# Soft-capped attention into an attention mixture: pairs of heads taken two by two, with one exponential for each two

## The chip, the core and the metric

The kernel runs on one NeuronCore of a Trainium2 chip. A core has five engines that run side by side, each through its own instructions in order: TensorE (PE in the profile, its weight loads PEld), VectorE (DVE), ScalarE (ACT), GpSimd (POOL) and SyncE (SP, which here issues most of the DMAs). They meet through semaphores. Matmul results go to PSUM, which has eight banks of 512 fp32 values on each of 128 partitions; everything else lies in SBUF. The metric is the device time of one execution in microseconds (us).

## The reference

There are two stages. The first is ordinary attention over 8 batches and 12 heads with 448 tokens and head size 64, whose scores are capped by a tanh. The second takes its result as x (448 tokens, 768 wide for each batch), runs four causal attention experts of head size 64 over it, and mixes the two experts that a gate picks for each token.

```python
scores = scale * np.matmul(q, k.transpose(0, 1, 3, 2))
scores = cap * np.tanh(scores / cap)                    # cap = 30
attn = np.exp(scores - np.max(scores, axis=-1, keepdims=True))
x = (attn / attn.sum(-1, keepdims=True)) @ v            # heads side by side
...
logits = x @ w_gate                                     # top 2 of 4 experts, softmax of the two
for e in range(E):
    q = x @ wq[e]; k = x @ wk[e]; v = x @ wv[e]
    a = softmax(causal(scale * (q @ k.transpose(0, 2, 1))))
    ye = a @ v @ wo[e]
    out += mask_e * w_e * ye
```

## The kernel before

The work of the first stage is cut into **pairs** of heads: 8 batches of 6 pairs make 48 pairs, numbered through. Pairs 42 to 47, the last batch, are computed for their first 320 tokens as pairs 42 to 47, and for the remaining 128 tokens of all six as two more units, 48 and 49, of three pairs each. The scores of a pair are seven blocks of 448 columns: keys 0 to 383 in three chunks of 128 for each of the two heads, which makes six blocks, and a **tail** with the last 64 keys of both heads.

For each pair, PE writes these blocks into PSUM (`heads`, L854, for the chunks, where the two heads run side by side on half the rows each; `tails`, L864). ACT applies the tanh from PSUM into an SBUF buffer `yp` (`tanh`, L907): three blocks from the **score tile** X, then two from Y, then two from Y again. The names of the three are X, Y1 and Y2. Then one exponential runs in place over all seven blocks, 3136 columns (`expo`, L919). PE multiplies the result by v (`pv`, L934 for the tail and L942 for the chunks), in four windows of 128 tokens and two PSUM banks; v carries a column of ones, so that the sum of the exponentials comes out beside the product. DVE divides (L965, L968). The pair's result is transposed, by PE or, from pair 36 on, by DMA, and stands as x for the second stage.

PSUM's eight banks are divided by hand: tile X has three, tile Y has two, and three banks, A0 to A2 (`AUX`), serve all other matmul results, one group of matmuls for each bank until DVE has read it. The second stage may use the banks of X where these are idle.

The second stage of batch b runs while ACT works on the pairs of the next batch. PE computes values and gate logits (L1088), keys and queries (L1096); POOL picks the experts and builds a mask (`g_`, `mB`), which a DMA transposes (`mT`) and DVE multiplies onto the queries (`qm`, L1170). `b_score` then writes scores for two experts into X, and ACT takes their exponential, 1024 columns, from there (L1301). This comes twice for a batch, at fixed pairs (`exps`): 5 and 6 pairs after the batch's end, or 4 and 6 for the last two of the seven batches handled so. Behind it come the product with the values (L1351), the weighting (L1366), the sum over experts on POOL (L1376), a transpose, and the output projection with `wo` (L1413), which `ob` carries to the output. The eighth batch's second stage, the end of the kernel, has code of its own, `last`.

What sets the order is a **planner** inside the kernel. `Graph.op` records each operation with its engine, a cost and its reads and writes; ACT's operations of the first stage form a fixed chain; `Graph.dues` gives every other operation a due time from that chain, and `Graph.solve` lists the operations of all engines by due time, cost and free banks, with corrections by hand or by search in the table `RANKS`. The result is one fixed order for each engine; on the chip, only semaphores decide when an instruction starts. `Group(banks)` stands for a result that needs one of these banks; `takes` and `frees` say which score banks an operation occupies or gives back.

The main loop goes over the pairs and calls, for pair p, in this order: X of p; Y1 of p; then the exponential of p - 1, what the second stage has due, PV and transpose of p - 1; then Y2 of p. So ACT runs tanh X, tanh Y1, exponential of the pair before, tanh Y2, and round again. `yp` has four buffers of seven blocks.

Of the kernel before, what the change touches and what calls it, by code (L numbers as in the profile page):

```python
# [26 lines left out]
        136: 93, 174: 305, 290: -418,  # L27
    }),
    (27.5, {
        507: 475,  # L30
    }),
    (67.5, {
        678: -572, 692: 231, 735: -81, 738: -31, 741: 513, 841: 473, 1112: 748, 1167: -284,
    }),
    (87.5, {
        716: 497, 727: -643, 760: -112, 767: -1037, 862: 1282, 888: 375, 919: 264,
    }),
    (127.5, {
        1092: 467, 1196: 214, 1239: -453, 1249: 345, 1267: 323, 1277: 281, 1398: -60, 1401: 289,
        1405: 243, 1449: -132, 1535: 337, 1537: 820,  # L40
    }),
    (147.5, {
        1338: 97, 1345: 117, 1355: 477, 1387: -702, 1413: 186, 1525: 119, 1548: -196,
    }),
    (167.5, {
        1600: 205, 1607: 294,
    }),
# [7 lines left out]
    }),  # L55
    (254.5, {
        2520: -331, 2577: -265, 2635: -902, 2645: 2133, 2659: 128, 2667: 486, 2678: 522, 2702:
        -188, 2703: -340, 2706: -238, 2713: -937, 2729: -581, 2766: 2204, 2788: 297,
# [3 lines left out]
TURN = 2.2  # L62
SAIL = 1.1
SHIP = 1.25
BEGIN = {"POOL": 0.8, "DVE": 0.9, "SP": 0.8, "ACT": 0.8, "PE": 1.25}
NWARM = 6
KEEP = 8
# [4 lines left out]
PDUE = 2.793  # L72
PSTEP = 11.594
# [3 lines left out]
KD = 34  # L77
NFILL = 35
# [10 lines left out]
class Group:  # L89


    def __init__(self, banks, hold=0.0):
        self.banks = banks
        self.hold = hold
        self.bank = None
        self.last = None


class Graph:
# [66 lines left out]
    def dues(self, when):  # L166


        for o in reversed(self.ops):
            d = INF  # L170
            if o.own is not None:
                d = o.own if not isinstance(o.own, tuple) else when[o.own[0].idx] + o.own[1]
            d = min(d, when.get(o.idx, INF))
            for s, late in o.succ:
                d = min(d, s.due - self.gap(o, s, late) - (0.1 if s.eng != o.eng else 0.0))
            o.due = d
        for o in self.ops:
            if o.opens:
                o.grp.due = o.due
            if o.grp is not None and not o.opens and o.grp.hold:  # L180
                o.due = min(o.due, o.grp.due + o.grp.hold)

    def solve(self, when, banks, lent):
# [21 lines left out]
        def pick(o, t):  # L205
            best = None
            for b in o.grp.banks:
# [3 lines left out]
                if b in taken and taken[b]:  # L211
                    continue
# [4 lines left out]
        def est(o, e):  # L217
# [114 lines left out]
def kernel(  # L332
# [50 lines left out]
    Y = pools["right"][0][1].tile([128, 2, 512], f32, name="Y")  # L383
    BANK = {f"A{i}": psum.tile([128, 512], f32, name=f"A{i}") for i in range(3)}
# [3 lines left out]
    for i in range(2):  # L388
        BANK[f"Y{i}"] = Y[:, i, :]
    XB = tuple(f"X{i}" for i in range(3))  # L390
    YB = tuple(f"Y{i}" for i in range(2))
    ANY = AUX + XB + YB

    PART = {"X": X[:, 0:2, :]}

    def apart(side, due, *parts):


        def fn():
            pools[side].pop()[0].__exit__(None, None, None)  # L400
            for tiles in parts:
                p = score_pool("p" + "".join(x for t in tiles for x in t), side)
                pools[side].append(p)
                for t in tiles:
                    w = p[1].tile([128, len(t), 512], f32, name="".join(t) + "s")
                    for i, x in enumerate(t):
                        BANK[x] = w[:, i, :]
                    if len(t) > 1:
                        PART["X"] = w

        bs = [x for tiles in parts for t in tiles for x in t]
        G.op("PE", 0.0, fn, (), [("s", x) for x in bs], 0.0, name="apart", due=due, takes=bs,
             frees=bs)
# [57 lines left out]
    yf = [sb(f"yp{i}", [128, 7 * S + 64]) for i in range(NYP)]  # L471
    yp = [t[:, 0 : 7 * S].rearrange("p (a s) -> p a s", s=S) for t in yf]
# [12 lines left out]
    qm = [[sb(f"qm{s}_{r}", [128, S]) for r in range(2)] for s in range(2)]  # L485
# [19 lines left out]
    p2 = yp[NPV % NYP].rearrange("p a s -> p (a s)")[:, 0 : E * 512].rearrange(  # L505
# [109 lines left out]
    def setup_b():  # L615
        def pad():
            for t in yf:
                nc.gpsimd.memset(t[:, 7 * S :], 1.0)
# [221 lines left out]

    def keysT(p):
        return qk[p % NQK][:, S:] if p < KD else kd[p // 2 % 3][:, p % 2]

    def heads(p, what):
        dst = X if what == "X" else Y
        ci = {"X": 0, "Y1": 1, "Y2": 2}[what]
        t, kT = qk[of(p, what)[0] % NQK], keysT(of(p, what)[0])
        n = wid(p)
        for c in (ci,) if p < NP else range(KC):
            for g in range(2):  # L850
                r = slice(64 * g, 64 * (g + 1))
                o, qs = (slice(0, n), slice(0, n)) if p < NP else (
                    slice(128 * c, 128 * (c + 1)), slice(W1, S))
                nc.tensor.matmul(  # L854
                    dst[:, g, o], kT[r, 128 * (c + 1) : 128 * (c + 2)], t[r, qs],
                    start=True, stop=True,
                )

    def tails(p):
        for i, m in enumerate(of(p)):  # L860
# [3 lines left out]
            nc.tensor.matmul(X[:, 2, o], keysT(m)[:, 0:128], t[:, qs], start=True, stop=True)  # L864

    def fill(p, what):
        def rd(p, what=None):
            return [y for m in of(p, what) for y in (
                ("qk", m % NQK, "k") if m < KD else ("kd", m // 2 % 3), ("qk", m % NQK, "q"),
                ("qkw", m % NQK))]  # L870

        bs = XB if what == "X" else YB
        both = [("s", bs[0]), ("s", bs[1])]
        if what == "X" and p and p - 1 not in alone:
            pass
        elif what == "Y2" and p < NPV - 1 and p not in alone:
            pe(0, lambda: (heads(p, "Y2"), heads(p + 1, "X")), rd(p, "Y2") + rd(p + 1, "X"),
               both + [("s", XB[0]), ("s", XB[1])], occ=0.01 + (wid(p) + wid(p + 1)) / 2400,
               name=f"sY2X_{p}", takes=YB + XB[0:2])
        else:  # L880
            pe(0, lambda: heads(p, what), rd(p, what), both, occ=0.008 + wid(p) / 2400,
               name=f"s{what}_{p}", takes=bs[0:2])
        if what == "X":
            if p == 0:
                tr_first_tails()
            pe(wid(p), lambda: tails(p), rd(p) + [
                ("qk", m % NQK, "t") if m < KD else ("kd", m // 2 % 3) for m in of(p)], [("s", bs[2])], name=f"sT_{p}",
               takes=bs[2:3])
# [7 lines left out]
    alone = {0, 1, *exps}  # L896
    ACTS = {}
    SL = {"X": (0, 3), "Y1": (3, 5), "Y2": (5, 7)}

    def tanh(p, what):  # L900
        y = yp[p % NYP]
        a, b = SL[what]
        src = X if what == "X" else Y
        bs = XB if what == "X" else YB
        fr = bs
        n = wid(p)
        ACTS[what, p] = act(c_act(n * (b - a)), lambda: nc.scalar.activation(  # L907
            y[:, a:b, 0:n], src[:, 0 : b - a, 0:n], AF.Tanh, scale=isc / capf),
            [("s", x) for x in bs], [("yp", p % NYP, what), ("tick", p, what)], fixed=True,
            name=f"t{what}_{p}",  # L910
            frees=fr)

    def expo(p, parts=(("X", "Y1", "Y2"),)):
        y = yp[p % NYP]
        for pt in parts:
            a, b = SL[pt[0]][0], SL[pt[-1]][1]
            ks = [("yp", p % NYP, x) for x in pt]
            n = wid(p)
            act(c_act(n * (b - a), False), lambda a=a, b=b, n=n: nc.scalar.activation(  # L919
# [3 lines left out]
    def pv(p):  # L923
        if p >= NP:
            return pv2(p)
        y = yf[p % NYP]
        u = p % NV
        SLOT = {0: (0, 1), 1: (3, 4), 2: (5, 6)}

        def mm(g, i, n, what):  # L930
            ps = bank(g)[:, 0 : 4 * (Dh + 1)].rearrange("p (n g d) -> p n g d", n=2, g=2)
            w = 256 * i + 128 * n if p >= NAT else WIN[2 * i + n]
            if "X" in what:
                nc.tensor.matmul(  # L934
                    ps[:, n, :, :], y[:, 2 * S + w : 2 * S + w + 128], vtz[u], start=(n == 0), stop=False,
                    skip_group_check=True,
                )
            cs = [c for c, x in enumerate(("X", "Y1", "Y2")) if x in what]
            for c in cs:
                for h in range(2):  # L940
                    o = SLOT[c][h] * S + w
# [917 lines left out]
```

## Time and profile before

| what | value |
|---|---|
| median of 3 runs | 305.61 us (304.93 to 306.35) |
| the profiled execution | 304.79 us |
| its span, first to last instruction | 303.1 us |
| granted TensorE clock | 1.000 |
| ACT busy | 290.2 us, 96% |
| PE busy (pipelined, ends modelled) | 282.0 us, 93% |
| DVE busy | 213.5 us, 70% |
| POOL busy | 189.4 us, 62% |
| tanh, 150 instructions (L907) | 101.7 and 68.3 us on Y and X |
| exponentials of the first stage, 51 (L919) | 142.4 us |

A row of the timeline has the start in us from the beginning of the span, the duration, the engine, the line in the code, the operation, what is written and read with its shape, and how many such rows were merged; in brackets stands idle time of the engine before it and what ended it. A row of the instruction groups has the busy time in all and the mean duration in ns, then the idle time before the group. In a row of the stages each engine's busy time is followed by the number of instructions, then come the granted clock, the DMA share and the rate. Durations of neighbouring ACT or PE rows overlap, so the distance from one start to the next is shorter than the duration.

### The profile page before, as it was taken

What the parts mean: (1) busy time and instruction counts of PE and PEld (TensorE: products, weight loads), DVE (VectorE), ACT (ScalarE), POOL (GpSimd) and SP (SyncE); (2) the same over time, 40 slices, a digit from 0 to 9 for tenths busy, and PEclk for the clock granted to TensorE, in tenths of its full rate; (3) what the DMA queues carried; (4) which work ended last, traced back from release to release, by engine and by line L of the source; (5) the groups of instructions that cost most, each with busy time, mean ns of one, the idle gap of its engine ahead of it and who ended that gap; (6) DMA issues with size and microseconds to landing.
All of it is one profiled execution on the core that took longest, in us unless ns stands there. A gap on an engine that the chain in (4) does not pass through costs nothing.

```text
span 303.1 us, 8955 instructions
## 1 busy us (share of the span) xinstructions
PE 282.0 (93%) x3470; PEld 188.1 (62%) x3470; DVE 213.5 (70%) x630; ACT 290.2 (96%) x244; POOL 189.4 (62%) x537
## 2 busy tenths in 40 slices
PE   7897989999999999999999999999898999989992
PEld 4463546666666676667666676656665675657771
DVE  3354556866867877687887887697766878486972
ACT  5999999999999999999999999999999999989981
POOL 6793435997699664958799355927469305711580
PEclk9999999999999999999999999999999999999999
DMA  6999999999993399677996874455028751743136
GB/s 168 223 206 238 236 233 298 284 225 281 264 233 88 118 257 244 161 216 194 280 197 170 235 244 123 55 151 146 2 52 123 216 92 21 103 142 93 37 151 215
DMA packets 86874, 53.12 MB, mean 175 GB/s; under 512 B 47536, under 2 KB 83120, under 8 KB 86832
## 3 DMA queue, kind: packets, MB, share of 16 engines
q1 hardware_dynamic: 86448, 52.13, 69.8%
q8 instruction: 27, 0.44, 0.6%
q10 hardware_dynamic: 384, 0.43, 0.5%
q14 instruction: 15, 0.12, 0.2%
HBM read 36.19 MB, written 11.01 MB: 156 GB/s over the span
## 4 chain that ended last, share of the span: by engine, by line
ACT 64%; PE 15%; POOL 5%; DMA 5%; DVE 5%; issue 4%; ACTq 0%; DVEq 0%; POOLq 0%
ACT yp L907 33%; ACT yp L919 28%; ACT pP L1301 3%; DMA mT<-mB 3%; PE A L1413 2%; PE X L1292 2%; PE A L1088 2%; PE Y L854 1%; DMA ktf<-in_k_dram 1%; PE A L942 1%; POOL oS L1376 1%; POOL mB L1248 1%; PE A L1479 1%; DMA oT<-oS 1%; PE A L1514 1%
## 5 line engine op out<-in xcount | busy, mean ns | idle before, releaser
L919 ACT ACTIVATE yp<-yp 128x3136 f16<-128x3136 f16 (+4 forms) x51 | 142.4, 2794 | 0.0
L907 ACT ACTIVATE yp<-Y 128x896 f16<-128x896 f32 (+2 forms) x100 | 101.7, 1017 | 1.3 <-PE Y L854 1.3
L907 ACT ACTIVATE yp<-X 128x1344 f16<-128x1344 f32 (+2 forms) x50 | 68.3, 1367 | 0.4 <-PE X L854 0.3
L942 PE MATMUL A<-v,yp 128*128 128x65 f16 x1008 | 49.8, 193 | 0.0
L942 PEld LDWEIGHTS <-yp 128*128 128x128 f16 x1008 | 43.6, 97 | 4.0 <-issue 2.1
L934 PE MATMUL A<-vtz,yp 128*128 128x130 f16 x168 | 37.3, 222 | 3.9 <-ACT yp L919 1.6
L744 POOL CAST v<-vf 128x384 f16<-128x384 f32 x48 | 24.6, 519 | 20.8 <-PE A L942 13.1
L968 DVE TENSOR_TENSOR xk<-A,rca 128x256 f16<-128x256 f32 x84 | 35.3, 421 | 2.2
L708 POOL CAST q<-qf 112x512 f16<-112x512 f32 x44 | 26.6, 618 | 13.7 <-PE A L758 9.0
L439 DVE COPY ob<-A 128x384 f32<-128x384 f32 (+1 forms) x50 | 25.6, 550 | 2.4 <-PE A L1413 2.0
L817 DVE COPY qk<-A 128x960 f16<-128x960 f16 x32 | 20.3, 652 | 9.2 <-PE A L758 9.0
L934 PEld LDWEIGHTS <-yp 128*128 128x128 f16 x168 | 16.2, 97 | 16.1 <-issue 8.8
L854 PE MATMUL Y<-qk 64*128 64x448 f16 x136 | 24.7, 357 | 1.5 <-ACT yp L907 0.9
L1366 DVE SCALAR_TENSOR_TENSOR oB<-A,rcb,mw 128x256 f16<-128x256 f32 x55 | 25.3, 477 | 1.0
L1311 POOL TENSOR_SCALAR_AFFINE_SELECT pP<-pP 128x384 f16<-128x384 f16 x14 | 7.4, 528 | 29.3 <-ACT pP L1301 29.3
L965 DVE RECIPROCAL rca<-A 128x4 f32<-128x4 f32 x84 | 15.0, 178 | 14.2 <-PE A L942 13.2
L1413 PE MATMUL A<-wo,oT 128*128 128x384 f16 x106 | 22.8, 326 | 1.0 <-DVE qm L1170 1.0
L1351 PE MATMUL A<-vB,pP 128*128 128x260 f16 x138 | 22.2, 274 | 1.3 <-DVE oB L1366 0.5
L1028 DVE COPY xT<-A 128x448 f16<-128x448 f16 (+1 forms) x38 | 14.7, 386 | 11.2 <-PE A L1019 10.8
L1088 PE MATMUL A<-wvg,xT 128*128 128x260 f16 x168 | 21.3, 274 | 0.6 <-DVE oB L1366 0.3
L1376 POOL TENSOR_TENSOR oS<-oB,oB 128x512 f16<-128x512 f16 x14 | 16.1, 1155 | 8.2 <-issue 5.0
L758 PE MATMUL A<-ident,q 112*128 112x112 f16 x192 | 19.8, 214 | 0.7 <-DVE oB L1366 0.4
(240 smaller groups left out, 620.2 us busy)
## 6 DMA issues: line engine op xcount, KB each, us to landing
qf<-in_q_dram SPq DMA_DIRECT2D x23, 448.0 KB, 5.7
kf<-in_k_dram SPq DMA_DIRECT2D x23, 384.0 KB, 5.0
vf<-in_v_dram SPq DMA_DIRECT2D x23, 384.0 KB, 4.7
out_dram<-ob SPq DMA_DIRECT2D x21, 384.0 KB, 3.1
ktf<-in_k_dram SPq DMA_DIRECT2D x46, 32.0 KB, 5.0
vtf<-in_v_dram SPq DMA_DIRECT2D x46, 32.0 KB, 4.3
out_dram<-ob SPq DMA_DIRECT2D x6, 192.0 KB, 2.9
ob<-in_moe_wv_dram SPq DMA_DIRECT2D x2, 384.0 KB, 4.8
```

The source lines that it names most:

```text
L439: (nc.scalar.copy if o.eng == "ACT" else nc.vector.tensor_copy)(dst(), src())
L708: e(q16[i], qf[s][:, h].rearrange("p h (c d) -> p c h d", c=QC))
L744: nc.gpsimd.tensor_copy(v16[u][:, :, :, 0:Dh], vf[s][:, h].rearrange("p h (c d) -> p h c d", c=KC))
L854: nc.tensor.matmul(dst[:, g, o], kT[r, 128 * (c + 1) : 128 * (c + 2)], t[r, qs], start=True, stop=True,)
L907: ACTS[what, p] = act(c_act(n * (b - a)), lambda: nc.scalar.activation(y[:, a:b, 0:n], src[:, 0 : b - a, 0:n], AF.Tanh, scale=isc / capf), ...
L919: act(c_act(n * (b - a), False), lambda a=a, b=b, n=n: nc.scalar.activation(y[:, a:b, 0:n], y[:, a:b, 0:n], AF.Exp, scale=capf), ks, ks, f ...
L934: nc.tensor.matmul(ps[:, n, :, :], y[:, 2 * S + w : 2 * S + w + 128], vtz[u], start=(n == 0), stop=False, skip_group_check=True,)
L942: nc.tensor.matmul(ps[:, n, h, :], y[:, o : o + 128], v16[u][:, h, c, :], start=False, stop=(c == 2), skip_group_check=True,)
L968: dve(c_dve(128 * m), lambda g=g, i=i, rc=rc, m=m: nc.vector.tensor_tensor(xk[p % NXK][:, 2 * i : 2 * i + m, :, :], view(g)[:, 0:m, :, 0:D ...
L1088: nc.tensor.matmul(bank(g)[:, 0 : E * Dh + E], xT[x][:, j, WIN[n] : WIN[n] + 128], wvg[:, j, :], start=(j == j1), stop=(j == jn),)
L1366: dve(c_dve(E * Dh) + 0.06, lambda g=g, k_=k_, n=n: nc.vector.scalar_tensor_tensor(oB[s][:, n, :, :], view(g)[:, :, 0:Dh], rcb[k_][:, 0, : ...
L1413: nc.tensor.matmul(bank(g)[:, 0 : D // 2], oT[x][:, n // 2, r, n % 2, :], wo2[r][:, c0:c1], start=(r == 0), stop=(r == 1),)
```

## The change

Both score tiles get three banks, X and Y, and only two banks, A0 and A1, stay reserved for other results. The tiles are used strictly in turn (`flip`). Pairs 0, 1 and 40 to 49 still run one by one with tanhs over three, two and two blocks. Pairs 2 to 39 run as 19 **doubles** (a, b) of fourteen blocks: five tanhs over two, three, three, three and three blocks, called X, Y1, Y2, Z1 and Z2, and one exponential over all fourteen, 6272 columns. The blocks of the two pairs are mixed: the third tanh carries the last two blocks of a and the tail of b, the fourth b's first two and one of its second, the fifth the rest. The exponential of the double before, and all that hangs on it, comes behind the first tanh of a double. The probability buffers become two of fourteen blocks.

Results of other matmuls may now use any bank: a `Brief` group may take a score bank that is idle, if the planner expects the next score there more than 2 us later (`LEND`). The planner holds score refills back to at most 2 us before they are due (`AHEAD`). The second stage's exponentials come 6 and 8 pairs after a batch's end for the first six batches, and 4 and 6 for the seventh; each such score goes to the tile whose turn it is, and a third buffer for masked queries is added. Planning constants (`TURN`, `PDUE`, `PSTEP`, due times of values and transposes) and the table `RANKS` are new, so the order on all engines is new.

```diff
-    Y = pools["right"][0][1].tile([128, 2, 512], f32, name="Y")
-    BANK = {f"A{i}": psum.tile([128, 512], f32, name=f"A{i}") for i in range(3)}
+    Y = pools["right"][0][1].tile([128, 3, 512], f32, name="Y")
+    BANK = {f"A{i}": psum.tile([128, 512], f32, name=f"A{i}") for i in range(2)}
...
-    yf = [sb(f"yp{i}", [128, 7 * S + 64]) for i in range(NYP)]
+    yf = [sb(f"yp{i}", [128, 14 * S + 64]) for i in range(2)]
...
-    qm = [[sb(f"qm{s}_{r}", [128, S]) for r in range(2)] for s in range(2)]
+    qm = [[sb(f"qm{i}_{r}", [128, S]) for r in range(2)] for i in range(3)]
...
-                if b in taken and taken[b]:
+                if b in taken and taken[b] and not (
+                        o.grp.brief and taken[b][0].due + lag > s + LEND):
                     continue
...
+            if o.takes and o.name != "apart" and o.due > START:
+                t = max(t, o.due + lag - AHEAD)
...
+    FIRST, SECOND = (0, 1, 4, 2, 3, 5, 6), (8, 9, 7, 10, 11, 12, 13)
...
-    XOFF = (5, 6)
-    late = {LB - 1: (4, 6), LB - 2: (4, 6)}
-    exps = {HP * (b + 1) + o: (b, s) for b in range(LB) for s, o in enumerate(late.get(b, XOFF))}
+    exps = {HP * (b + 1) + o: (b, s) for b in range(LB) for s, o in enumerate(
+        XOFF if b < LB - 1 else (4, 6))}
...
-            g = Group(AUX)
+            g = Brief(ANY)
...
-        for part, bk in ((H1, "X1"), (H0, "X0")):
+        z = flip()
+        for part, bk in ((H1, z + "1"), (H0, z + "0")):
...
+    units = [(0,), (1,)] + [(p, p + 1) for p in range(2, DUO, 2)] + [(p,) for p in range(DUO, NPV)]
...
+            z = flip()
+            fill(z, (a, 0))
+            go("X", z, 2, 0)
+            ACTS["Y1", a] = ACTS["X", a]
+            behind(unit, prev, ACTS["X", a])
+            z, z2 = flip(), flip()
+            if a in exps:
+                fill(z, (a, 1))
+                fill_tail(z, a)
+                go("Y1", z, 3, 2)
+                fill(z2, (a, 2))
+                fill_tail(z2, b)
+            else:
+                fill(z, (a, 1), join=(z2, (a, 2)))
+                fill_tail(z, a, (z2, b))
+                go("Y1", z, 3, 2)
+            go("Y2", z2, 3, 5)
+            z = flip()
+            fill(z, (b, 0), (b, 1, (0,), 2))
+            go("Z1", z, 3, 8)
+            z = flip()
+            fill(z, (b, 1, (1,), 0), (b, 2, (0, 1), 1))
+            go("Z2", z, 3, 11)
```

More of the change, by code (lines that the diff above doesn't have):

```diff
@@ L71 @@
 PJ = 4
[L72 to L73 removed]
+PDUE = 12.0
+PSTEP = 0.8
 HEAD = 12.0
@@ L94, in __init__, with Brief @@
         self.hold = hold
+        self.brief = False
         self.bank = None
         self.last = None
+def Brief(banks, hold=0.0):
+    g = Group(banks, hold)
+    g.brief = True
+    return g
 class Graph:
@@ L863, in tails @@
                 slice(128 * i, 128 * (i + 1)), slice(W1, S))
[L864 to L888, printed above, removed]
@@ L913, in expo, with tanh @@
[L913 to L919, printed above, removed]
+    def tanh(p, what, z, k, lo, keys):
+        y = yp[p // 2 % 2]
+        bs = ZB[z][0:k]
+        n = wid(p)
+        ACTS[what, p] = act(c_act(n * k), lambda: nc.scalar.activation(
+            y[:, lo : lo + k, 0:n], TILE[z][:, 0:k, 0:n], AF.Tanh, scale=isc / capf),
+            [("s", x) for x in bs], keys + [("tick", p, what)], fixed=True,
+            name=f"t{what}_{p}", frees=bs)
@@ L1744, with warmth, behind @@
     load(1, 1)
-    for p in range(NPV):
+    units = [(0,), (1,)] + [(p, p + 1) for p in range(2, DUO, 2)] + [(p,) for p in range(DUO, NPV)]
+    def warmth(p, what):
+        if 0 < p < KEEP:
+            for _ in range(KEEPN):
+                g = Group(AUX)
+                pe(512, lambda g=g: nc.tensor.matmul(
+                    bank(g)[:, 0:512], warm[:, 0:128], warm[:, 0:512], start=True, stop=True),
+                   ["warm", ("tick", p, what)], ["warmps"], g, name="fill")
+    def behind(unit, prev, ref):
+        expo(prev[-1])
+        p = unit[0]
+        if p in exps:
+            b_score(*exps[p])
+        for i, m in enumerate(prev):
+            pv(m)
+            xt(m, (ref, XDUE[len(prev) - 1] + XSTEP * i))
+        if p == HP * (LB - 1) + PJ:
+            b_half(LB - 1, ref)
+        if p % HP == 0 and p < NP:
+            bb = p // HP - 1
+            b_v(bb, ref)
+            if bb < MD:
+                b_qk(bb, ref)
+            b_gate(bb)
+            b_mask(bb, 0)
+            if bb < MD:
+                b_gate1(bb)
+                b_gexp(bb)
+            b_mask(bb, 1)
+            if bb >= MD:
+                b_qk(bb, ref)
+                b_gate1(bb)
+                b_gexp(bb)
+            b_gate2(bb)
+        if p in exps:
+            bb, s = exps[p]
+            b_pv(bb, s)
+            if s == 1:
+                b_ot(bb)
+                b_wo(bb, ref, *((21.59, 1.8) if bb < LB - 1 else (21.884, 0.5)))
+    prev = None
+    for unit in units:
+        p = unit[0]
         if p == 1:
```

361 lines of the change are left out of this document (195 added, 166 removed), and 15 rows, old and new, of the table RANKS.

## The prediction

> **What bounds the kernel now.** I read the page first (busy time, slices, chain), then the timeline of ACT and the differences between successive starts, then PE's timeline beside it.
>
> ```profile
> span 303.1 us, 8955 instructions
> ...
> PE 282.0 (93%) x3470; PEld 188.1 (62%) x3470; DVE 213.5 (70%) x630; ACT 290.2 (96%) x244; POOL 189.4 (62%) x537
> ...
> ACT  5999999999999999999999999999999999989981
> ...
> ACT 64%; PE 15%; POOL 5%; DMA 5%; DVE 5%; issue 4%; ACTq 0%; DVEq 0%; POOLq 0%
> ```
>
> ACT is busy in nearly all slices and carries most of the chain. PE is also at 93%, but its rows overlap, so that figure says little; its real price per matmul is the distance to the next start (below). An ACT row is longer than its distance to the next start too. I therefore price ACT by starts.
>
> ```profile
> 16.92 2.82 ACT L919 ACTIVATE yp<-yp 128x3136 f16<-128x3136 f16 x1
> 19.63 0.92 ACT L907 ACTIVATE yp<-Y 128x896 f16<-128x896 f32 x1
> 20.43 1.30 ACT L907 ACTIVATE yp<-X 128x1344 f16<-128x1344 f32 x1
> 21.60 0.94 ACT L907 ACTIVATE yp<-Y 128x896 f16<-128x896 f32 x1
> 22.39 2.85 ACT L919 ACTIVATE yp<-yp 128x3136 f16<-128x3136 f16 x1
> ...
> 256.47 2.10 ACT L919 ACTIVATE yp<-yp 128x2240 f16<-128x2240 f16 x1
> 258.43 0.73 ACT L907 ACTIVATE yp<-Y 128x640 f16<-128x640 f32 x1
> ```
>
> One pair takes 2.71 + 0.80 + 1.17 + 0.79 = 5.47 us of ACT, back to back. Nothing that shortens another engine helps here unless ACT stands still. It does so in two kinds of place. The first is where the second stage's exponential (1024 wide, L1301) borrows score tile X and X must be refilled within one 0.80 us tanh:
>
> ```profile
> 76.21 1.17 ACT L907 ACTIVATE yp<-Y 128x896 f16<-128x896 f32 x1
> 77.07 1.49 ACT L907 ACTIVATE yp<-X 128x1344 f16<-128x1344 f32 x1
> ...
> 103.76 1.24 ACT L1301 ACTIVATE pP<-X 128x1024 f16<-128x1024 f32 x1
> 104.68 1.12 ACT L907 ACTIVATE yp<-Y 128x896 f16<-128x896 f32 x1
> 105.61 1.38 ACT L907 ACTIVATE yp<-X 128x1344 f16<-128x1344 f32 x1
> ...
> 238.56 1.08 ACT L907 ACTIVATE yp<-Y 128x896 f16<-128x896 f32 x1
> 239.73 1.29 ACT L907 ACTIVATE yp<-X 128x1344 f16<-128x1344 f32 x1
> ```
>
> The 0.80 step became 0.86 in the first and 1.17 in the last of six such places (of eleven with 448-wide pairs; the other five lose nothing): 0.06, 0.13, 0.12, 0.13, 0.26 and 0.37. The second is late: the score for the first exponential of the seventh batch (pair 46) is not there in time.
>
> ```profile
> 264.43 2.16 ACT L919 ACTIVATE yp<-yp 128x2240 f16<-128x2240 f16 x1
> 267.43 1.02 ACT L1301 ACTIVATE pP<-X 128x1024 f16<-128x1024 f32 x1 [0.85 <-PE X L1292]
> 268.35 0.70 ACT L907 ACTIVATE yp<-Y 128x640 f16<-128x640 f32 x1
> 269.38 0.97 ACT L907 ACTIVATE yp<-X 128x960 f16<-128x960 f32 x1 [0.33 <-PE X L854]
> ```
>
> The exponential stepped 3.00 us where its shape takes 1.96 (the rows at 256.47 and 258.43), so 1.0 is lost, and 0.4 more behind it.
>
> **The change, part by part.** *Fewer ACT instructions.* The elements stay the same; what goes is the fixed part. For the exponential, 896 elements more cost 2.71 - 1.96 = 0.75 us, 0.837 ns each, so of 2.71 us 0.085 are fixed. For the tanh, 448 more cost 1.17 - 0.80 = 0.37, 0.826 ns each, and 0.06 are fixed. Each of the 19 doubles (pairs 2 to 39) has one exponential and one tanh less: 19 x 0.145 = **-2.75 us**. The readings are good to 0.01, which moves the fixed parts by 0.035, so -2.1 to -3.4. ACT is the path here, so this counts in full as long as ACT stays fed.
>
> [...]
>
> *The refill behind the second stage's exponential.* With X and Y both of three banks and used in turn, that exponential takes the tile that is wanted one tanh later, and that tanh is now 1.17 long, not 0.80. The first five losses lie in the doubles and go: **-0.7 us** (0 to -0.7). The sixth is at pair 40, outside them; pairs 40 and up keep the old pattern, so I leave it. What is late next is the refill itself, in the next item.
>
> *Three-bank refills.* Now the last tanhs of a double and the first of the next each need the tile that was released one tanh before. Of 19 doubles, 9 have three such refills and 10, with an exponential of the second stage, have four: 67, of which 48 fill three banks. A bank more costs one more step of 0.19 on PE:
>
> ```profile
> 100.62 0.35 PE L864 MATMUL X<-qk 128*128 128x448 f16 x1
> 100.81 0.44 PE L1292 MATMUL X<-qm,kB 128*128 128x256 f16 x4
> ...
> 104.28 0.22 PE L934 MATMUL A<-vtz,yp 128*128 128x130 f16 x1
> ...
> 104.52 0.22 PE L934 MATMUL A<-vtz,yp 128*128 128x130 f16 x1
> ...
> 105.20 0.36 PE L854 MATMUL X<-qk 64*128 64x448 f16 x2
> ```
>
> The two-bank refill at 105.20 follows the exponential that ended at 105.00, takes 0.36, and the tanh starts at 105.61. Seen by starts, the eleven refills of this kind needed between 0.80 or less (five) and 1.17. With 0.19 more they need 0.99 or less to 1.36, against a window of 1.17: only the slowest two would be late, by 0.08 and 0.19. That is 0.025 in the mean of eleven, times 48: **+1.2 us**; 0 if PE is always there, +2.2 if all behave like the six slow ones. The 19 two-bank refills have the window that Y has today, which shows no loss at 16.92 to 22.39: nothing. Between two refills the new order on PE mostly holds two PV windows, 0.24 each by the rows at 104.28 and 104.52, plus the refill's 0.38: 0.86 of 1.17.
>
> *Second stage two pairs later.* Between the last exponential of pair 41, on which the seventh batch's chain starts, and the exponential at 267.43, one more second-stage exponential (0.90, the step at 103.76 to 104.68 is 0.92) now stands on ACT. The chain gains that much time: of the 1.4 us lost there I take back **-0.9** (0 to -1.4, or +1 if the sixth batch's later work delays the chain).
>
> *The tail.* PE's order shows what pays for this. In the kernel before, all eight output projections (wo) of the sixth batch stand before the last score refill. After it, six of them stand behind that refill, and more of the seventh batch's PV too.
>
> ```profile
> 102.46 0.81 PE L1413 MATMUL A<-wo,oT 128*128 128x384 f16 x4
> 103.11 0.61 PE L1292 MATMUL X<-qm,kB 128*128 128x64 f16 x10
> ...
> 280.49 2.45 ACT L919 ACTIVATE yp<-yp 128x2688 f16<-128x2688 f16 x1
> 282.82 0.81 ACT L907 ACTIVATE yp<-Y 128x768 f16<-128x768 f32 x1
> 283.51 2.54 ACT L919 ACTIVATE yp<-yp 128x1920 f16<-128x1920 f16 x2
> ...
> 280.80 0.34 PE L854 MATMUL Y<-qk,kd 64*128 64x128 f16 x6
> ...
> 286.38 0.35 PE L1050 MATMUL X2s<-v,yp 128*128 128x65 f16 x6
> 286.66 0.25 PE L1567 MATMUL Y0s<-qB,kB 64*128 64x192 f16 x1
> ...
> 290.00:294.00 4.00, 3.80 (x54) 2.43 (x52) 3.40 (x15) 3.38 (x9) 3.51 (x17) 1.00 0.42 167
> ```
>
> From the last refill (280.80) to the end of the last pairs' PV (286.66) PE has 5.86 us today, while ACT's last exponentials end at 286.05. By column counts at the steps above (448 columns 0.19, a PV window 0.24) its work there is 22 matmuls of 260 columns (2.4), six of 320 (0.8), six row-halved scores (0.3), the refill (0.2) and six PV windows (1.4): 5.1, so 0.8 is slack. The new order puts six wo pairs (four matmuls in 0.65, so 0.33 each: 2.0), five PV matmuls of 260 columns (0.11 each: 0.55) and some 0.6 of transposes and key projections between the same two points: +3.1. Less the slack, 2.3. Behind that point PE's order holds 0.2 less, and keys and queries of the last tokens are read out one behind the other on DVE, where today the queries come 0.9 behind the keys:
>
> ```profile
> 290.35 0.37 ACT L439 CAST kL<-X1s 128x256 f16<-128x256 f32 x1 [1.19 <-PE X1s L1661]
> ...
> 291.26 0.41 DVE L439 CAST qL<-X1s 128x256 f16<-128x256 f32 x1
> ```
>
> A readout is 0.41, so 0.5 comes back: **+1.6 us** (0 to +3.5; the upper end with the same gaps, nothing back and seven more readouts, since DVE is at 3.40 of 4.00 there).
>
> *Without cost.* The probability buffers (two of 14 slots) are overwritten by a double's first tanh 4 tanhs, 4.7 us, after the exponential; the four PV windows of the pair in question are 0.96 and stand ahead of that: covered, up to +0.96 a double if PV slips. DVE's and the DMA queue's instruction counts do not change; pair data are wanted up to one exponential (2.7 us) earlier, and no tanh waits for a load in the stretches shown. The third mask buffer and six fewer warming matmuls cost nothing: PE has room between refills.
>
> **Sum.** -2.75 - 0.7 + 1.2 - 0.9 + 1.6 = -1.55. The profiled execution took 304.79 us (span 303.1 and 1.7 around it), 0.8 under the median of 305.61; against its own time the sum gives 303.2, against the median **304.0 us**.
>
> **Rivals.** *The tail hides its added work* (faster). PE's gaps before 286.66 and the waits at the end take it in; then -3.15 stands: 302.5. For it: ACT's main part ends earlier and the moved work has slack later. Against: DVE's 3.40 of 4.00.
>
> *The tail takes everything* (no change): +3.5 there, which leaves +0.35: 306.0. For it: PE's order, fixed beforehand, puts the moved work ahead of the last PV.
>
> *Two free banks are too few* (slower). Matmul results other than scores have A0 and A1 in place of three banks while the tanhs run, since both score tiles are taken; they are lent only in the long exponential. A PV group is 0.48 on PE, then a reciprocal and a multiply on DVE hold its bank:
>
> ```profile
> L968 DVE TENSOR_TENSOR xk<-A,rca 128x256 f16<-128x256 f32 x84 | 35.3, 421 | 2.2
> L965 DVE RECIPROCAL rca<-A 128x4 f32<-128x4 f32 x84 | 15.0, 178 | 14.2 <-PE A L942 13.2
> ```
>
> That is about 1.2 us a turn, 0.6 a group with two banks; six or seven groups stand in the 4.7 us of tanhs, 3.6 to 4.2. It fits, narrowly, but PE is in order: a group that waits for its bank delays the refill behind it. If each of the 67 refills is late by 0.1 beyond its margin, +6.7 replaces +1.2: 309.5. From 0.065 each (4.3 in all), the whole is slower by 0.5%. [...] The trace of before has three and shows hardly a loss; none here shows two.
>
> **How the numbers follow.** Within 0.5% is within 1.5 us, about what a measurement here can tell. Forecast (303.0 to 305.0): 0.32, of it 0.20 faster, 0.12 the same. Hidden tail 0.26, faster. Tail takes everything 0.14, the same. Two banks too few 0.28, of it 0.26 slower and 0.02 the same. So faster 0.46, same 0.28, slower 0.26. The range takes in the hidden tail with its refills free (1.2 less: 301.3) and the nearer part of the slow rival: 301.2 to 308.0.
>
> **What would show it.** ACT groups: 131 tanhs in place of 150, 32 exponentials in place of 51, the long one stepping 5.3 us. The tanh behind a second-stage exponential without a loss; three-bank tanhs stepping 1.17 to 1.19, where a mean above 1.23 means the slow rival, with PE rows waiting for DVE. The last exponential ending near 282.9 rather than 286.05, and the end 1.6 us farther behind it than now. It is wrong if ACT's main part shows new gaps of more than 3 us, or the tail is as long as before.

## The result, and the profile after

The changed kernel takes 347.13 us in the median (346.55 to 348.0), the kernel before 305.43 us beside it: a ratio of 1.136 (95% interval 1.133 to 1.140). It is 42 us slower. The prediction said 304.0, with a range up to 308.0.

The page of the changed kernel: span and instructions, PE's busy row, the slices of ACT, and the chain by engine.

```profile
span 345.4 us, 8965 instructions
...
PE 288.2 (83%) x3464; PEld 190.8 (55%) x3464; DVE 216.6 (63%) x629; ACT 293.1 (85%) x207; POOL 189.2 (55%) x535
...
ACT  5889999799997798998997699977998788878672
...
PE 38%; ACT 20%; DVE 13%; DMA 10%; SPq 7%; issue 5%; POOL 5%; ACTq 0%; DVEq 0%; POOLq 0%
```

Every engine is busy for about as long as before: ACT for 293.1 us against 290.2, PE for 288.2 against 282.0. All of them stand still more. ACT was full in nearly every slice and is now below nine tenths in 22 of 40. The chain that ends last has moved from ACT (64% before, 20% now) to PE (15% before, 38% now), DVE (5% and 13%) and others.

Where ACT runs, it runs as forecast. The timeline of ACT in a double without a second-stage exponential:

```profile
25.18 1.29 ACT L952 ACTIVATE yp<-Y 128x1344 f16<-128x1344 f32 x1
26.37 0.91 ACT L952 ACTIVATE yp<-X 128x896 f16<-128x896 f32 x1
27.17 5.43 ACT L963 ACTIVATE yp<-yp 128x6272 f16<-128x6272 f16 x1
32.49 1.29 ACT L952 ACTIVATE yp<-Y 128x1344 f16<-128x1344 f32 x1
```

The steps are 1.19, 0.80 and 5.32 us. The groups of ACT instructions show where it stands still, in the changed kernel and then in the one before:

```profile
L952 ACT ACTIVATE yp<-X 128x1344 f16<-128x1344 f32 (+4 forms) x67 | 76.0, 1134 | 11.0 <-PE X L904 5.5 <-PE X L1396 1.3 <-PE X L1458 0.9
L952 ACT ACTIVATE yp<-Y 128x1344 f16<-128x1344 f32 (+4 forms) x64 | 72.7, 1136 | 12.0 <-PE Y L904 5.1 <-PE Y L913 2.2 <-PE Y L984 1.4
L1346 ACT ACTIVATE pP<-Y 128x1024 f16<-128x1024 f32 x8 | 8.2, 1020 | 5.4 <-PE Y L913 3.9 <-POOL g_h L1243 0.8 <-DVE rcb L1409 0.7
L1346 ACT ACTIVATE pP<-X 128x1024 f16<-128x1024 f32 x6 | 6.1, 1023 | 9.7 <-PE X L913 6.8 <-DVE rcb L1409 1.5 <-DVE xk L1040 1.1
```

```profile
L907 ACT ACTIVATE yp<-Y 128x896 f16<-128x896 f32 (+2 forms) x100 | 101.7, 1017 | 1.3 <-PE Y L854 1.3
L907 ACT ACTIVATE yp<-X 128x1344 f16<-128x1344 f32 (+2 forms) x50 | 68.3, 1367 | 0.4 <-PE X L854 0.3
L1301 ACT ACTIVATE pP<-X 128x1024 f16<-128x1024 f32 x14 | 16.3, 1167 | 0.9 <-PE X L1292 0.9
```

Between the two bars of a row stand busy time and mean, behind the second the idle time and what ended it. Before, the tanhs and the second-stage exponentials had 1.3, 0.4 and 0.9 us of idle time; now their four groups have 11.0, 12.0, 5.4 and 9.7. Two things in the rows of the changed kernel are odd. The second-stage exponential L1346 reads banks 0 and 1 of a score tile, yet most of its waiting (6.8 and 3.9 us) is ended by L913, the tail score, which goes to bank 2. And tanhs over banks 0 and 1 wait for the output projection (L1458) and second-stage products (L1396), which are lent other banks.

A count over all of ACT's starts gives the balance. Against the step that each shape takes where nothing delays it (0.80, 1.17, 2.71, 5.32 us and so on), ACT's instructions lose 43.9 us in the changed kernel and 3.6 in the one before. The fixed work on ACT is 2.7 us less (275.0 and 272.3), the stretch from the last exponential to the end is 4.4 us longer (17.0 before, 21.4 now), and the first tanh starts 0.3 later: 40.3 - 2.7 + 4.4 + 0.3 = 42.3 us, the difference of the spans.

### The profile page after: what moved, and what is told of

The parts are those of the page before. It is cut to its first block, busy times and chain, and to the rows that moved or that the text cites. A ratio compares the mean times of both kernels' runs of the same rounds, so it can differ in the third digit from the quotient of the medians.

```text
span 345.4 us, 8965 instructions
## 1 busy us (share of the span) xinstructions
PE 288.2 (83%) x3464; PEld 190.8 (55%) x3464; DVE 216.6 (63%) x629; ACT 293.1 (85%) x207; POOL 189.2 (55%) x535
## 4 chain that ended last, share of the span: by engine, by line
PE 38%; ACT 20%; DVE 13%; DMA 10%; SPq 7%; issue 5%; POOL 5%; ACTq 0%; DVEq 0%; POOLq 0%
ACT yp L952 15%; DMA qf<-in_q_dram 8%; SPq L588 3%; PE A L1137 3%; DVE ob L471 3%; ACT pP L1346 3%; PE A L984 3%; PE X L1137 3%; DVE oB L1411 3%; PE Y L904 3%; PE X L904 2%; PE A L1129 2%; ACT yp L963 2%; SPq L687 2%; PE X L1458 2%
## 5 line engine op out<-in xcount | busy, mean ns | idle before, releaser
L963 ACT ACTIVATE yp<-yp 128x6272 f16<-128x6272 f16 (+5 forms) x32 | 132.0, 4128 | 0.0
L952 ACT ACTIVATE yp<-X 128x1344 f16<-128x1344 f32 (+4 forms) x67 | 76.0, 1134 | 11.0 <-PE X L904 5.5
L952 ACT ACTIVATE yp<-Y 128x1344 f16<-128x1344 f32 (+4 forms) x64 | 72.7, 1136 | 12.0 <-PE Y L904 5.1
L984 PEld LDWEIGHTS <-yp 128*128 128x128 f16 x1008 | 44.5, 99 | 9.2 <-issue 8.7
L984 PE MATMUL A<-v,yp 128*128 128x65 f16 x876 | 44.0, 195 | 0.0
L1009 DVE TENSOR_TENSOR xk<-A,rca 128x256 f16<-128x256 f32 x73 | 30.7, 422 | 2.0
L725 POOL CAST k<-kf 128x384 f16<-128x384 f32 x33 | 16.5, 511 | 12.2 <-PE A L800 8.1
L904 PE MATMUL Y<-qk 64*128 64x448 f16 x102 | 19.3, 370 | 0.7 <-DVE qk L849 0.3
L904 PE MATMUL X<-qk 64*128 64x448 f16 x102 | 19.0, 363 | 0.9 <-DVE kB L1124 0.4
L1129 PEld LDWEIGHTS <-xT 128*128 128x128 f16 x168 | 15.8, 97 | 4.8 <-issue 2.4
L1337 PEld LDWEIGHTS <-kB 128*128 128x128 f16 x252 | 15.0, 98 | 6.3 <-issue 4.6
L790 PEld LDWEIGHTS <-q 112*128 112x128 f16 x192 | 14.9, 100 | 6.4 <-issue 3.4
L1396 PEld LDWEIGHTS <-pP 128*128 128x128 f16 x140 | 12.4, 97 | 9.2 <-issue 6.1
```

Source lines behind the costliest of these rows:

```text
L790: nc.tensor.transpose(ps[:, 0:S].rearrange("m (g c t) -> m c g t", c=QC, t=16)[:, c], q16[i][:, c, :, :].rearrange("p h d -> p (h d)"), id ...
L904: nc.tensor.matmul(dst[:, bank0 + g - gs[0], 0:n], keysT(p)[r, 128 * (c + 1) : 128 * (c + 2)], qk[p % NQK][r, 0:n], start=True, stop=True)
L952: ACTS[what, p] = act(c_act(n * k), lambda: nc.scalar.activation(y[:, lo : lo + k, 0:n], TILE[z][:, 0:k, 0:n], AF.Tanh, scale=isc / capf), ...
L963: act(c_act(n * (b - a), False), lambda a=h + a, b=h + b: nc.scalar.activation(y[:, a:b, 0:n], y[:, a:b, 0:n], AF.Exp, scale=capf), ks, ks ...
L984: nc.tensor.matmul(ps[:, n, h, :], y[:, o : o + 128], v16[u][:, h, c, :], start=False, stop=(c == 2), skip_group_check=True,)
L1009: dve(c_dve(128 * m), lambda g=g, i=i, rc=rc, m=m: nc.vector.tensor_tensor(xk[p % NXK][:, 2 * i : 2 * i + m, :, :], view(g)[:, 0:m, :, 0:D ...
```

## The experiments

### What one stretch shows

Behind the double (16, 17) the second stage of the second batch is due. Here are ACT, DVE and PE of the changed kernel in that stretch:

```profile
111.06 5.44 ACT L963 ACTIVATE yp<-yp 128x6272 f16<-128x6272 f16 x1
118.71 1.02 ACT L1346 ACTIVATE pP<-X 128x1024 f16<-128x1024 f32 x1 [2.21 <-PE X L913]
...
113.11 0.56 DVE L471 COPY ob<-X 128x384 f32<-128x384 f32 x1 [0.25 <-PE X L1458]
...
114.80 0.39 DVE L1308 TENSOR_TENSOR qm<-qB,X 128x448 f16<-128x448 f16 x1 [0.36 <-PE X L1458]
...
111.94 0.49 PE L1458 MATMUL X<-wo,oT 128*128 128x384 f16 x2
...
112.59 0.49 PE L1458 MATMUL X<-wo,oT 128*128 128x384 f16 x2
...
113.72 0.38 PE L1303 MATMUL X<-ident,mB 128*128 128x128 f16 x4 [0.43 <-DVE ob L471]
...
115.70 0.49 PE L1458 MATMUL X<-wo,oT 128*128 128x384 f16 x2 [0.29 <-DVE ob L471]
...
117.88 0.61 PE L1337 MATMUL X<-qm,kB 128*128 128x256 f16 x8 [0.60 <-DVE ob L471]
118.32 0.35 PE L913 MATMUL X<-qk 128*128 128x448 f16 x1
```

The first output product (111.94) goes to bank 0 of X and ends at 112.43. DVE could read it then (it is idle from 112.86), but starts at 113.11, just after the next product on X (112.59), which goes to bank 1. The mask transposes (113.72) go to bank 2, which nobody holds, and start when DVE has read bank 0. So it goes on, a step on PE, a step on DVE, until the exponential, which needs banks 0 and 1, waits for the tail score in bank 2.

The semaphores in the program say the same. Each wait names the instruction that it waits for, and the operands name the banks. Some 185 waits of the changed kernel are for an instruction in the same tile X or Y that shares no bank with the waiting one (75 on PE, about 70 on DVE and 40 on ACT). The kernel before has none. So the framework that sets the semaphores orders accesses to one PSUM tile also where they touch different banks, while the planner gives each bank a time of its own. Before, nothing but scores and second-stage scores used X and Y while the tanhs ran, and the rule cost nothing. Lending their banks to other results made it count.

This became the theory 'whole tile'. Its rivals: 'tight plan' (two own banks, refills held back, no reserve) and 'long exponential' (PE has no probabilities for 5.3 us).

### The banks ordered apart

The order of all instructions stays. In short: for each two that touch X or Y without a bank in common, on different engines and with no other tile in common, the framework is told to set no wait.

```diff
     for o in order:
         o.fn()
+    for ins in the program, in order:
+        for old in earlier instructions on the same tile X or Y:
+            if old.engine != ins.engine and not (banks(ins) & banks(old)) and no other tile is shared:
+                tc.declare_no_dep(ins, old, reason="other bank")
```

> The changed kernel, same order on every engine, but an instruction on one bank of X or Y no longer waits for one on another bank of the same tile (pairs that share no bank and no other tile). Theory 'whole tile' (the lent banks are slices of two tiles of three banks, and each access is ordered against the last one anywhere in its tile, while the planner counts each bank for itself): nearly all of the loss goes, 301 to 308 us, ACT idle in front of the tanh under 8 us. Rival 'tight plan' (two aux banks and refills held back leave no reserve, whatever the tracking): above 320 us. Rival 'long exponential' (PE has no probabilities for 5.3 us): above 320 us.

Measured: 309.22 us (308.39 to 310.76), 1.0146 of the kernel before (1.0100 to 1.0192). 38 of the 42 us are gone with the same work in the same order. Its page, and its groups of ACT:

```profile
span 306.9 us, 8986 instructions
...
ACT  4989999999999999999999999999999999999771
```

```profile
L952 ACT ACTIVATE yp<-X 128x1344 f16<-128x1344 f32 (+4 forms) x67 | 80.0, 1194 | 2.0 <-PE X L904 1.6
L952 ACT ACTIVATE yp<-Y 128x1344 f16<-128x1344 f32 (+4 forms) x64 | 76.2, 1190 | 2.7 <-PE Y L904 2.2 <-PE Y L984 0.4
L1346 ACT ACTIVATE pP<-Y 128x1024 f16<-128x1024 f32 x8 | 8.8, 1094 | 0.0
L1346 ACT ACTIVATE pP<-X 128x1024 f16<-128x1024 f32 x6 | 6.2, 1035 | 0.4 <-PE X L1337 0.4
```

The idle time of 11.0, 12.0, 5.4 and 9.7 us has become 2.0, 2.7, 0.0 and 0.4. The same stretch as above, ACT, DVE and PE:

```profile
104.80 5.60 ACT L963 ACTIVATE yp<-yp 128x6272 f16<-128x6272 f16 x1
110.85 1.02 ACT L1346 ACTIVATE pP<-X 128x1024 f16<-128x1024 f32 x1 [0.44 <-PE X L1337]
...
106.69 0.55 DVE L471 COPY ob<-X 128x384 f32<-128x384 f32 x1
...
105.84 0.49 PE L1458 MATMUL X<-wo,oT 128*128 128x384 f16 x2
...
107.04 0.39 PE L1303 MATMUL X<-ident,mB 128*128 128x128 f16 x4
...
110.20 0.61 PE L1337 MATMUL X<-qm,kB 128*128 128x256 f16 x8
```

The transposes follow the first output product after 1.20 us, not 1.78, and the last second-stage scores after 4.36, not 5.94. The exponential waits for its own scores and no longer for the tail. Both rivals expected over 320 us, and both fall as explanations of the main loss.

The times show what the dropped waits cost; that such waits can be left out of any kernel they do not show.

### Which of the waits matter

The same, with one condition more: only where the waiting instruction is on ACT, or only where it is not.

```diff
-            if old.engine != ins.engine and ...
+            if ins.engine == ACT and old.engine != ins.engine and ...      # the one
+            if ins.engine != ACT and old.engine != ins.engine and ...      # the other
```

> The same orderings dropped only where the waiting instruction is on ACT (a tanh or a second-stage exponential that waits for a neighbouring bank). Theory 'whole tile': part of the loss goes, since ACT's own late waits sum to 22 us in the trace of after, but PE and DVE still wait for each other: 320 to 338 us. Rivals 'tight plan' and 'long exponential': 343 to 349 us.

> The same orderings dropped only where the waiting instruction is on PE or DVE; ACT still waits for the neighbouring bank. Theory 'whole tile': part of the loss goes, 315 to 335 us, and with the run that frees ACT alone it adds up to more than the whole loss or about it. Rivals: 343 to 349 us.

Measured, with one execution each: 335.04 us with ACT freed alone, 313.69 with PE and DVE freed alone. Against 347.13 that is 12.1 and 33.4 us, together 45.5 against 37.9 for both. The second is below the range that was expected for it. The rows of L1346 on X, first with ACT freed alone, then with PE and DVE freed alone:

```profile
L1346 ACT ACTIVATE pP<-X 128x1024 f16<-128x1024 f32 x6 | 6.1, 1023 | 7.1 <-PE X L1337 7.1
```

```profile
L1346 ACT ACTIVATE pP<-X 128x1024 f16<-128x1024 f32 x6 | 6.1, 1024 | 0.9 <-PE X L913 0.8
```

With ACT freed alone, L913 is gone as releaser, but 7.1 of the 9.7 us of waiting stay, now for the exponential's own scores: most of the time had been lost upstream. With PE and DVE freed, the scores are there, and the wait for the tail is 0.8 us. So most of the loss is the ping-pong of PE and DVE, and ACT's wait for a neighbouring bank is mostly its last link. The idle time that the profile put down to L913 was therefore not the price of that wait.

### The long exponential in two

```diff
-            act(..., lambda: nc.scalar.activation(y[:, a:b, 0:n], y[:, a:b, 0:n], AF.Exp, scale=capf), ...)
+            act(..., lambda: [nc.scalar.activation(
+                y[:, s : min(s + 7, b), 0:n], y[:, s : min(s + 7, b), 0:n], AF.Exp, scale=capf)
+                for s in range(a, b, 7)], ...)
```

> The changed kernel with the exponential of each double (14 blocks, 5.3 us) issued as two of 7 blocks, one behind the other in the same place; all orderings kept. Rival 'long exponential': the first pair's probabilities come 2.7 us earlier, so PE has work in the gap, 325 to 338 us. Theory 'whole tile' and rival 'tight plan': 19 more instructions on ACT at 0.145 us each are 2.75 us, of which a part is hidden by the stalls: 345 to 350 us.

> The kernel with the banks apart, the exponential of each double in two of 7 blocks. Theory 'dry PE': the probabilities of the first pair come 2.7 us earlier, PE's gaps before 45 us and the halved clock go, which gives back up to 2.2 us of the 2.75 that 19 more instructions on ACT cost: 309 to 310.5 us. Rival 'the long exponential costs nothing': 311.5 to 312.2 us. Rival 'it costs much' (more than early on): under 308 us.

In the changed kernel: 346.06 us in one execution, 1.1 less than with one exponential. With the banks apart: 310.81 us, 1.0202 of the kernel before (1.0182 to 1.0223), 1.6 us slower than with one exponential by the medians and 1.7 by the ratios.

Both expectations took 2.75 us as the cost of the 19 instructions. That is the price of an exponential and a tanh together; the split adds exponentials alone. Two steps of 2.706 us in place of one of 5.320 are 0.09 more, 19 times, and so 1.7 us. So in the changed kernel the split gives back at most some 3 of the 42 us, and little of the loss hangs on the length of the exponential. With the banks apart it gives back next to nothing: that is the rival 'the long exponential costs nothing', which at the right price expects 310.9 us. (In the profiled execution ACT's late starts sum to 0.9 us less, but the first tanh starts 0.4 later.) 'Dry PE' is not supported in its form: the clock is still below full (0.79 from 12 to 20 us, 0.89 from 20 to 36), and PE's gaps before 45 us are still there (1.74 and 2.66 us). They have only moved behind the products, in front of scores that wait for a free tile, as this row of PE shows:

```profile
43.54 0.54 PE L904 MATMUL X<-qk 64*128 64x448 f16 x3 [2.66 <-ACT yp L952]
```

### What is left with the banks apart: the start

With the banks apart, 3.9 us against the kernel before remain in the spans of the profiled executions (306.95 and 303.08), 4.4 in the medians. The balance of the spans: ACT's fixed work -2.7, first tanh +0.2, late starts on ACT +2.9 where the instruction ahead of the late one starts before 60 us and +0.3 where it starts later, tail +3.1.

About half of the 2.9 us goes with TensorE's clock. Stages of the kernel before, and of the one with the banks apart (the clock is the third figure from the right):

```profile
12.00:20.00 8.00, 6.77 (x79) 3.94 (x78) 4.27 (x11) 8.00 (x6) 6.76 (x35) 1.00 0.89 203
...
44.00:50.00 6.00, 5.94 (x55) 3.80 (x53) 3.42 (x14) 6.00 (x6) 1.56 (x4) 1.00 1.04 299
```

```profile
12.00:20.00 8.00, 7.01 (x54) 3.92 (x55) 2.83 (x7) 8.00 (x6) 7.46 (x39) 0.57 0.87 213
...
44.00:50.00 6.00, 5.73 (x60) 3.36 (x58) 4.52 (x11) 5.56 (x4) 2.13 (x5) 0.77 0.45 134
```

PE issues 54 matmuls where it issued 79, at half the clock for most of the stretch (0.57 in the mean). Where this first dip begins, PE has just waited 1.08 us for POOL (`ktz`, L770), and no double has had its exponential yet. Ahead of the second dip PE has nothing to do while the exponential runs:

```profile
41.59 0.23 PE L977 MATMUL A<-vtz,yp 128*128 128x130 f16 x1 [2.46 <-ACT yp L963]
```

The experiment puts work on the constant tile into the three largest gaps:

```diff
         o.fn()
+        for _ in range({152: 4, 272: 6, 440: 9}.get(o.idx, 0)):    # into a bank that no one holds
+            nc.tensor.matmul(BANK[spare][:, 0:512], warm[:, 0:128], warm[:, 0:512], start=True, stop=True)
```

> The kernel with the banks apart (e1_banks_apart, 309.2 us, PE still for 1.1, 1.8 and 2.5 us before 45 us, granted clock 0.5 from 12 to 20 us and from 44 to 46), with 19 more 512-column matmuls on the constant tile in these three gaps (4, 6 and 9), nothing else. Theory 'dry PE': PE has nothing to do until the exponential of a double ends, the clock is halved behind it, and the tanhs at 19.8, 43.7 and 56.4 us come 1.06, 0.64 and 0.54 us late for that: clock 1.0 throughout, 1.5 to 2.7 us faster than the kernel with the banks apart, so 306.3 to 308.0 us. Rival 'input comes late' (the DMA share is over 0.9 there): clock 1.0, but the same tanhs as late as before, 308.5 to 310 us.

Measured: 307.63 us (307.31 to 309.86), 1.0108 of the kernel before (1.0079 to 1.0137). The same two stages:

```profile
12.00:20.00 8.00, 6.96 (x91) 3.93 (x90) 3.69 (x10) 8.00 (x6) 7.08 (x39) 1.00 0.71 158
...
44.00:50.00 6.00, 4.95 (x60) 3.36 (x57) 3.06 (x12) 6.00 (x4) 2.54 (x6) 1.00 1.00 253
```

The clock is full, and the last exponential ends 1.3 us earlier (285.49 against 286.80). The tanhs behind those at 19.8 and 43.7 us, which started 1.06 and 0.64 late, come in time, and ACT's late starts of this early part sum to 1.6 us less. The third that was named, and the tanh after the next exponential, are as late as before at full clock (0.53 and 0.54), so their cause is another: 'dry PE' holds for two of its three tanhs. These are the two with the banks apart:

```profile
58.08 0.92 ACT L952 ACTIVATE yp<-Y 128x896 f16<-128x896 f32 x1 [0.42 <-PE Y L984]
...
64.76 1.29 ACT L952 ACTIVATE yp<-X 128x1344 f16<-128x1344 f32 x1 [0.44 <-PE X L904]
```

The first overwrites a probability buffer and waits until PE's last product (L984) has read it; so do the tanhs at 69.79 and 139.61, which lose 0.22 and 0.35. In the program this wait names a product that reads block 13 of the buffer, while the tanh overwrites blocks 0 and 1. So an order by whole tile may cost something here too; that was not tried. The second waits for a refill (L904, 64.35) that stands behind key projections in lent banks of X (L1137) and their readout on DVE (63.62 to 64.24).

The times agree (1.6 us less by the medians, 1.2 by the ratios), but the two intervals overlap, so the gain rests on the trace. This is the best version seen, and it does not beat the kernel before.

### What is left: the tail

> The kernel with the banks apart without the six output products of the sixth batch (L1458, two matmuls each) that stand behind the last refill, and without their evictions; that part of the output is left out. Theory 'tail' (these six are what makes the stretch from the last exponential to the end 20.15 us in place of 17.02): 2 to 3.2 us faster than with them, 306 to 307.3 us. Rival: PE has room for them there, or another chain sets the end: 308.4 to 309.5 us.

```diff
+    late = the six wo5 operations behind the last refill
     for o in order:
-        o.fn()
+        if o.idx not in late and o.idx - 1 not in late:
+            o.fn()
```

Measured: 309.13 us, 1.0144 of the kernel before (1.0112 to 1.0177): no different from the kernel with them. From the last exponential to the end it is 19.73 us, against 20.15 with them and 17.02 before. The six products are not what makes the tail longer; the rival is right. ACT's rows at the turn into the tail, first with the banks apart, then without the six products:

```profile
284.23 2.57 ACT L963 ACTIVATE yp<-yp 128x1920 f16<-128x1920 f16 x2
286.83 0.47 ACT L471 COPY ob<-Y2s 64x384 f32<-64x384 f32 x1
...
290.33 0.44 ACT L1622 ACTIVATE pP<-Y1s 128x320 f16<-128x320 f32 x1
```

```profile
284.98 2.57 ACT L963 ACTIVATE yp<-yp 128x1920 f16<-128x1920 f16 x2
...
290.24 0.44 ACT L1622 ACTIVATE pP<-Y1s 128x320 f16<-128x320 f32 x1 [1.19 <-PE A L1612]
```

The last batch's first exponential (L1622) starts 3.5 us after the last pair's has ended, and 2.7 after it without the six products. Before, it followed at once (the last pair's exponential ended at 286.05):

```profile
285.94 0.45 ACT L1577 ACTIVATE pP<-Y0s 128x320 f16<-128x320 f32 x1
```

With the banks apart its scores (L1612, 289.85) come behind the last batch's queries, whose second half PE projects (L1571) from 287.65 on; before, it did so (L1526) from 282.10 on. Of these 5.55 us the transpose of pair 47's result, on which the projection rests, accounts for 3.0: it stands at 282.50, before at 279.46. The rest is the order on PE, which is never idle in between: all values of the last batch (L1585) and products of the last pairs (L1091) now stand ahead of the queries. Which of the changes to the order pushed that chain back was not tried and stays open.

## Why the prediction was wrong, point by point

- **The step that failed** is one that the prediction took for granted where it counted banks one by one: in *Three-bank refills* and in the third rival, a result that is lent a score bank was held up by that bank alone. The program orders lent results by tile. With the banks apart the time is 309.2 us, and 38 of the 42 us belong to this point. Most of it also sits where the prediction saw no pressure: the third rival called the long exponential the time when banks are lent, and priced only the refills between tanhs (+1.2, or +6.7 in that rival). Of the 44 us that ACT's instructions lose in the changed kernel, 28 are lost by the instruction right behind an exponential.
- *Fewer ACT instructions*, -2.75: right. ACT's fixed work fell by 2.7 us, in the changed kernel as in the others with its shapes, 131 tanhs and 32 exponentials, the long one stepping 5.32.
- *Three-bank refills*, +1.2: right in size once the banks are apart. Of the 58 three-bank tanhs after 70 us 9 step more than 1.2 us; the mean is 1.191, and all together lose 1.2 us, of which 0.35 is the wait for a probability buffer at 139.61. In the changed kernel itself the mean was 1.246, the sign that was named for the slow rival.
- *Refill behind the second stage's exponential*, -0.7, and *two pairs later*, -0.9: with the banks apart ACT loses 0.2 us from 260 us on, where the kernel before lost 1.7, so the second gain came and was larger. The first came too: behind the ten second-stage exponentials inside the doubles, the tanhs from the tile that was borrowed start 0.1 us late in all. New losses take its place. From 60 to 260 us ACT loses 3.6 us against 1.7 before: 1.6 in front of tanhs that follow a three-bank tanh, 0.7 because the second-stage exponential at 110.85 is late itself, and 0.6 because the tanh right behind such an exponential is late at 147.03 and 159.22 (0.39 and 0.16); the rest is in small pieces.
- *Without cost*: wrong by 2.9 us. 1.6 of them hang on the clock, since filling three gaps brought them back (the clock went from 0.57 to 1.00 between 12 and 20 us, and from 0.77 to 1.00 between 44 and 50). The prediction looked for room on PE and found it; the room was the trouble. The six warming matmuls fewer may have their part: between 6.5 and 14 us there are 17, where the kernel before had 31, and the first dip follows there. The probability buffers were called covered; the wait for one costs 0.5 us at 58.08, and 0.6 at two places after 60 us. The refill at 64.76 is another 0.5.
- *The tail*, +1.6: right in sign, 3.1 with the banks apart (inside the bounds given), wrong in its account. The six output products, from which it was worked out, are worth 0.4 us there.
- The rival *two free banks are too few*, 309.5 us, comes near the time with the banks apart, but that is chance: the refills lose 1.2 us there, not 6.7. Its mechanism is not what these runs show.

With the banks apart, the terms of the sum would have come to -2.7 + 0.2 + 2.9 + 0.3 + 3.1 = 3.8 us: slower even so. The forecast of a gain rested on an early part and a tail that cost 2.9 and 1.5 us more than was thought.

## What to carry to other kernels

Before results share a multi-bank PSUM tile, find out how the framework orders accesses to it: a hand-written order that treats banks as independent does not hold if the semaphores join them (38 of the 42 us here), and the wait row gives it away, by naming a line that writes a bank the waiting instruction never reads. A long idle row in front of the bottleneck engine names the last link; freeing that engine alone gave back 12 us here, freeing the two engines behind it 33. And an engine with room to spare is not always an advantage: ask what its clock does around a gap (here 0.57 from 12 to 20 us, and 1.00 with work put into the gaps).

## What the runs showed of the hardware

With the banks apart the granted clock falls at 12.57 us, rises at 19.40, falls at 43.29 and rises at 46.70. It was 0.50 from 14 to 18 and from 44 to 46 us, and 1.00 from 20 to 42 us.

The longer of two gaps on PE was not always the one with the lower clock behind it. The kernel with the banks apart and the one without the six products run the same order up there, with the same two gaps ahead of PE's products: 1.77 us from 29.0 or 29.2 on, and 2.5 us from 39.1 or 40.1 on. In the first kernel the clock stays behind the shorter gap and falls behind the longer one. In the second kernel it is the other way round. The clock in the 40 slices of the span, 7.67 and 7.68 us each, first with the banks apart, then without the six products:

```profile
PEclk9879989999999999999999999999999999999999
```

```profile
PEclk9989799999999999999999999999999999999998
```

The fifth digit, from 30.7 us on, is 9 and 7; the sixth, from 38.4 on, is 8 and 9; the seventh is 9 in both. Stages of the second kernel around the two gaps (PE's busy time in us is the figure behind the comma, the clock the third from the right):

```profile
28.13:31.54 3.41, 1.14 (x22) 0.66 (x20) 1.73 (x4) 3.41 (x2) 0.96 (x2) 1.00 1.18 252
31.54:34.96 3.42, 3.42 (x37) 1.89 (x33) 2.13 (x8) 3.02 (x3) 0.54 (x2) 0.50 1.03 193
...
38.37:41.78 3.41, 1.75 (x10) 0.40 (x8) 0.89 (x2) 3.41 (x1) 1.23 (x4) 1.00 1.04 285
```

The shorter gap lies in a stretch with PE busy for 1.14 of 3.41 us, and half the clock follows. Most of the longer one lies in a stretch with PE busy for 1.75 of 3.41 us, and the clock stays. What decides between the two was not shown.
